# A fused attention and softplus feed-forward kernel: a list scheduler in place of a hand-interleaved order, and three weight phases in place of two

## The chip, the cores and the metric

The kernel runs on one core of a Trainium2 chip. The metric is the device time of one execution in microseconds: the median of the kernel's runs. The profiled execution is one more run, taken by the hardware profiler; its span goes from the first to the last instruction.

The engines are called by these names: TensorE (PE in the profile, PEld for its weight loads), VectorE (DVE), ScalarE (ACT), GpSimd (POOL) and SyncE (SP), which here only issues DMAs. Each engine works through its own instructions in program order and waits on semaphores for the others.

## The reference

```python
# q, k, v: (8, 8, 576, 64) float32; g_norm: (64,)
kv  = np.einsum('bhsd,bhse->bhde', k, v)
out = np.einsum('bhsd,bhde->bhse', q, kv)
rms = np.sqrt(np.mean(out * out, axis=-1, keepdims=True) + 1e-06)
x   = (out / rms * g_norm).transpose(0, 2, 1, 3).reshape(4608, 512)
# w_in: (512, 2048), w_out: (2048, 512), both float64
h   = x @ w_in
g   = np.maximum(h, 0.0) + np.log1p(np.exp(-np.abs(h)))   # softplus
return (g @ w_out).astype(np.float32)
```

The attention is linear: one 64 x 64 matrix kv for each batch and head, then q times it, and a norm over the 64 elements of a head.

## The kernel before

**Attention.** The 4608 tokens are 36 tiles of 128. For each of the 8 batches, `kv_part` (L240) accumulates k^T v of two heads at a time over the batch's 4.5 tiles in one PSUM bank; the two diagonal blocks are copied to `kv_diag`. For each tile, `turn_q` transposes q on TensorE (tp, L251) and ScalarE copies it out (qT, L253); `rows_out` (o, L262) multiplies it with `kv_diag`, ScalarE squares (L266), VectorE sums (L268), GpSimd raises to the power -1/2 (L269, L270), and `rows_norm` scales (L275). `turn_x` transposes the result (xp, L281), ScalarE multiplies it by g_norm (xg, L283), and x^T is stored in DRAM.

**Feed-forward.** Tokens are taken in 12 blocks of 384, d_ff in 16 chunks of 128. Each fp32 operand is divided into factors that TensorE multiplies in its fast fp32r mode: three for x^T (`split_x`, xv, L295 to L297), three for each weight (`divide` or `redivide`), three for g. A *step* is one chunk of one block: mm1 (L353) makes 128 x 384 of h with 12 matmuls; ScalarE computes softplus and the first factor (L358, L359), VectorE the other two (L360, L361): this is gv; mm2 (L373) adds gv's product with w_out to three sums of 128 x 512, one PSUM bank each, with 9 matmuls. There are 12 x 16 = 192 steps.

**Weights.** They arrive as float64. `conversion` makes fp32 of them in 128 x 512 halves (for each chunk a w_in half, j even, and a w_out half, j odd): six instructions of VectorE and three of ScalarE, then `divide`: one more on VectorE, three on ScalarE, and on TensorE the pair wd (L177, L178). Only eight chunks' factors fit in SBUF. So there are two phases of eight chunks: the first goes over all blocks with chunks 0 to 7, and leaves its sums in DRAM (ot, L379, the store L381); the second reads x^T and those partial sums again (L302, L390), adds them (L384) and writes the output (L386). Chunks 8 to 15 are converted during the first phase, spilled to DRAM, reloaded at the phases' turn and divided there by `redivide`.

**What sets the order.** Everything is written out by hand with `manual_schedule`. `attention` and `conversion` are generators; the main code advances them by given counts between the steps. While the first block's eight steps run, they start at fixed places among the conversions of the sixteen halves (`STARTS`, L440: step 0 with half 5, step 7 with half 15); after that each step advances the attention and the second half's conversions by one or two pieces. mm2 follows mm1 by `LAG = 2` steps. PSUM has two banks for mm1 and wd (tag h), three sums, and three banks (tag a) that kv, tp, o and xp share; when the attention is done, these three become a second set of sums (`ps_b`).

Of the kernel before, what the change touches and what calls it, by code (L numbers as in the profile page):

```python
# [8 lines left out]
F32 = mybir.dt.float32  # L9
# [9 lines left out]
P = 128  # L19
# [5 lines left out]

@with_exitstack
def kernel(
# [20 lines left out]

    nc = tc.nc
# [10 lines left out]
    CH = KF // 2  # L60
    LAG = 2
# [3 lines left out]
    wts = ctx.enter_context(tc.tile_pool(name="wts", bufs=1))  # L65
    dram = ctx.enter_context(tc.tile_pool(name="dram", bufs=1, space=DRAM))
    xpool = ctx.enter_context(tc.tile_pool(name="xpool", bufs=2))
    gpool = ctx.enter_context(tc.tile_pool(name="gpool", bufs=3))
    tmp = ctx.enter_context(tc.tile_pool(name="tmp", bufs=2))
    ps_h = ctx.enter_context(tc.tile_pool(name="ps_h", bufs=2, space=PSUM))  # L70
    ps_o = [ctx.enter_context(tc.tile_pool(name="ps_o", bufs=1, space=PSUM))]
    first_stack = ExitStack()
    ps_a = first_stack.enter_context(tc.tile_pool(name="ps_a", bufs=3, space=PSUM))
    att = first_stack.enter_context(tc.tile_pool(name="att", bufs=2))
    conv = first_stack.enter_context(tc.tile_pool(name="conv", bufs=1))

    ident_r = const.tile([P, P], F32R, name="ident_r")
    minus_r = const.tile([P, P], F32R, name="minus_r")
    ident = ident_r.bitcast(F32)
# [7 lines left out]

    wide = moe_w_in.dtype != F32
    raws, w_in_r, w_out_r, w_spill = {}, {}, {}, {}
# [11 lines left out]
    def fetch(j):  # L101
        src = w_source(j)
        dt, words = (U32, 2) if wide else (F32, 1)
        raws[j] = conv.tile([P, d_model, words], dt, tag="raw", bufs=2, name="raw")
        nc.sync.dma_start(
            out=raws[j].rearrange("p n w -> p (n w)").rearrange("p (a f) -> p a f", a=src.shape[1]), in_=src)

    def conversion(js, end):
# [8 lines left out]
        js = list(js)  # L117
        last = iter(())
        for j in js:
            raw = raws[j]  # L120
            w = conv.tile([P, d_model], F32, tag="w", name="w")
            if wide:
                lo, hi = raw[:, :, 0], raw[:, :, 1]
                t, p = (conv.tile([P, d_model], U32, tag=n, name=f"c_{n}") for n in "tp")
                tf, pf = t.bitcast(F32), p.bitcast(F32)
                lf = conv.tile([P, d_model], F32, tag="lf", name="lf")
                sq, junk = (conv.tile([P, d_model], BF16, tag=n, name=n) for n in ("sq", "junk"))
                nc.scalar.activation(sq, raw.bitcast(BF16)[:, :, 3], func=AF.Square, scale=2.0 ** 47)
                nc.scalar.activation(lf, lo, func=AF.Copy, scale=2.0 ** -52)
                nc.vector.tensor_scalar(out=t, in0=hi, scalar1=3, scalar2=0x3FFFFFF8,  # L130
                                        op0=ALU.logical_shift_left, op1=ALU.bitwise_and)
                yield
                nc.vector.scalar_tensor_tensor(out=t, in0=hi, scalar=0xC0000000, in1=t,
                                               op0=ALU.bitwise_and, op1=ALU.bitwise_or)
                raws.pop(j)
                if j + 2 <= js[-1]:
                    fetch(j + 2)
                yield
                yield from last
                nc.vector.scalar_tensor_tensor(out=tf, in0=sq, scalar=2.0 ** 64, in1=tf, op0=ALU.is_ge, op1=ALU.mult)  # L140
                nc.scalar.activation(junk, sq, func=AF.Identity, scale=2.0 ** -126, bias=big,
                                     accum_out=over[:, j:j + 1])
                yield
# [384 lines left out]
```

## Time and profile before

| | before |
|---|---|
| median of 3 runs | 1051.72 us (1051.38 to 1051.89) |
| the profiled execution's own time | 1047.91 us |
| its span | 1046.0 us |
| TensorE busy | 959.1 us, 92% |
| VectorE, ScalarE busy | 518.5 us, 424.8 us |
| DMA | 110.18 MB, 105 GB/s over the span |

A row of the groups reads: line, engine, operation, what is written <- what is read, shapes, count | busy us in all, mean ns of one | idle time of the engine just before them, and who ended it. One fp32 matmul is two instructions for kv and o (hence x8 for four matmuls), and one for the others. A row of a table by stretches reads: from and to in us, length, then busy us and instructions of TensorE, its weight loads, VectorE, ScalarE and GpSimd, TensorE's granted clock, the share of time in which the DMA engines moved data, and GB/s. The page's GB/s row gives equal slices of the span or of the window asked for.

### The profile page before, as it was taken

To read this page: it belongs to the slowest core of one execution; us is meant where nothing else is said; L and a number is where in the kernel's file an instruction comes from. 1 tells how busy PE (TensorE), PEld (TensorE's weight loads), DVE (VectorE), ACT (ScalarE), POOL (GpSimd) and SP (SyncE) were. 2 spreads that over 40 slices of the span, in tenths; PEclk is the share of its full clock that TensorE was granted. 3 is DMA by queue.
4 is the path that set the end of the run, shared out by engine and by line. 5 is a ranking of instruction groups with operands and counts; after the bars stand their busy time and mean duration, and the time that the engine had idled before them with its cause. 6 is when DMAs were issued, how large, how long until landed. Compare 5 with 4: busy or idle time off the path is not lost. (4 is left out here: it accounts for less than half of the span.)

```text
span 1046.0 us, 13139 instructions
## 1 busy us (share of the span) xinstructions
PE 959.1 (92%) x4994; PEld 861.4 (82%) x4994; DVE 518.5 (50%) x892; ACT 424.8 (41%) x834; POOL 88.3 (8%) x78
## 2 busy tenths in 40 slices
PE   4756768999998999989999999999999999999998
PEld 3646557898897978879898999899999999999997
DVE  3656754455464554546543457544443544444432
ACT  2546654444344443444532369333222322232221
POOL 0121112022021111113100000000000000000000
PEclk8587888999999999999999999999999999999999
DMA  9855544545555364443220333122211222022210
GB/s 220 186 151 137 139 121 121 153 121 161 143 139 143 99 161 117 126 119 104 100 65 16 101 114 108 52 90 91 81 51 51 91 91 81 25 77 91 81 61 31
DMA packets 158767, 110.18 MB, mean 105 GB/s; under 512 B 117104, under 2 KB 125296, under 8 KB 158704
## 3 DMA queue, kind: packets, MB, share of 16 engines
q1 hardware_dynamic: 158704, 109.34, 37.6%
q8 instruction: 39, 0.64, 0.3%
q14 instruction: 24, 0.20, 0.1%
HBM read 76.81 MB, written 32.51 MB: 105 GB/s over the span
## 5 line engine op out<-in xcount | busy, mean ns | idle before, releaser
L373 PE MATMUL op<-w,gv 128*128 128x512 f32 x1728 | 440.0, 398 | 11.2 <-ACT ot L379 11.2
L353 PE MATMUL hp<-xv,w 128*128 128x384 f32 x2304 | 439.5, 339 | 0.4 <-ACT g L358 0.4
L353 PEld LDWEIGHTS hp<-xv,w 128*128 128x128 f32 x2304 | 412.6, 189 | 16.6 <-ACT g L358 0.9
L373 PEld LDWEIGHTS op<-w,gv 128*128 128x128 f32 x1728 | 319.1, 189 | 73.2 <-ACT ot L379 14.2
L360 DVE TENSOR_TENSOR gv<-g,gv 128x384 fp32r<-128x384 f32 x192 | 107.1, 558 | 449.5 <-ACT gv L359 447.9
L358 ACT ACTIVATE g<-hp 128x384 f32<-128x384 f32 x192 | 94.1, 490 | 472.1 <-PE hp L353 470.6
L361 DVE SCALAR_TENSOR_TENSOR gv<-gv 128x384 fp32r<-128x384 f32 x192 | 107.2, 558 | 6.7
L359 ACT ACTIVATE gv<-g 128x384 fp32r<-128x384 f32 x192 | 100.8, 525 | 6.0
L270 POOL TENSOR_TENSOR r<-r,half 128x8 f32<-128x8 f32 x36 | 70.6, 1962 | 3.0
L240 PE MATMUL kv<-v_t,k_t 128*128 128x128 f32 (+1 forms) x320 | 55.1, 328 | 12.4 <-DMA v_t<-in_v_dram 12.4
L240 PEld LDWEIGHTS kv<-v_t,k_t 128*128 128x128 f32 (+1 forms) x320 | 51.1, 237 | 15.7 <-issue 13.8
L269 POOL TENSOR_SCALAR r<-r 128x8 f32<-128x8 f32 x36 | 17.0, 472 | 421.0 <-DVE r L268 421.0
L297 DVE SCALAR_TENSOR_TENSOR xv<-xv 128x512 fp32r<-128x512 f32 x72 | 49.8, 692 | 2.5
L262 PE MATMUL o<-kv_diag,qT 128*128 128x128 f32 (+1 forms) x320 | 46.3, 304 | 2.0 <-DVE sq L275 2.0
L296 DVE TENSOR_TENSOR xv<-xt,xv 128x512 fp32r<-128x512 f32 x69 | 47.3, 685 | 1.9 <-ACT xv L295 1.5
L262 PEld LDWEIGHTS o<-kv_diag,qT 128*128 128x128 f32 (+1 forms) x320 | 43.5, 205 | 4.1 <-DVE sq L275 2.5
L295 ACT ACTIVATE xv<-xt 128x512 fp32r<-128x512 f32 x69 | 42.8, 620 | 0.0
L178 PE MATMUL wd<-w,minus_r 128*128 128x512 f32 x16 | 10.8, 672 | 33.6 <-ACT w L174 33.6
L268 DVE TENSOR_REDUCE r<-sq 128x8 f32<-128x512 f32 x36 | 24.5, 681 | 28.8 <-ACT sq L266 28.5
L379 ACT ACTIVATE ot<-op 128x512 f32<-128x512 f32 x36 | 20.3, 593 | 43.9 <-DMA part<-ot 43.9
L251 PE MATMUL tp<-ident_r,q_t 128*128 128x128 f32 x144 | 25.5, 308 | 13.4 <-ACT xg L283 13.4
L178 PEld LDWEIGHTS wd<-w,minus_r 128*128 128x128 f32 x16 | 4.0, 250 | 38.8 <-ACT w L174 38.8
(50 smaller groups left out, 479.4 us busy)
## 6 DMA issues: line engine op xcount, KB each, us to landing
xt<-x SPq DMA_DIRECT2D x69, 256.0 KB, 2.8
x<-xg SPq DMA_DIRECT2D x36, 256.0 KB, 2.2
part<-ot SPq DMA_DIRECT2D x36, 256.0 KB, 2.2
pt<-part SPq DMA_DIRECT2D x36, 256.0 KB, 3.8
out_dram<-ot SPq DMA_DIRECT2D x36, 256.0 KB, 2.1
raw<-in_moe_w_in_dram SPq DMA_DIRECT2D x16, 512.0 KB, 4.6
k_t<-in_k_dram SPq DMA_DIRECT2D x32, 256.0 KB, 3.5
v_t<-in_v_dram SPq DMA_DIRECT2D x32, 256.0 KB, 4.2
```

The source lines that it names most:

```text
L240: nc.tensor.matmul(kvs[b][:, p], lhsT=kts[t][r0:r0 + n, 2 * p:2 * p + 2].rearrange("r h d -> r (h d)"), rhs=vts[t][r0:r0 + n, 2 * p:2 * p ...
L262: nc.tensor.matmul(o[r0:r0 + n, 2 * p:2 * p + 2].rearrange("r h d -> r (h d)"), lhsT=qT[:, p, r0:r0 + n], rhs=kv_diag[b % 2][:, p], start= ...
L270: nc.gpsimd.tensor_tensor(out=r, in0=r, in1=half, op=ALU.pow)
L295: nc.scalar.activation(xv[:, 0], x, func=AF.Copy, scale=DOWN)
L296: nc.vector.tensor_tensor(out=xv[:, 1], in0=x, in1=f32[:, 0], op=ALU.subtract)
L297: nc.vector.scalar_tensor_tensor(out=xv[:, 2], in0=f32[:, 1], scalar=-RADIX, in1=f32[:, 0], op0=ALU.mult, op1=ALU.add)
L353: nc.tensor.matmul(hp, lhsT=w[:, i, kd * P:(kd + 1) * P], rhs=xv[:, i, kd], start=(m == 0), stop=(m == 3 * KD - 1))
L358: nc.scalar.activation(g, hp, func=AF.Softplus, scale=1.0 + E)
L359: nc.scalar.activation(gv[:, 0], g, func=AF.Copy, scale=DOWN)
L360: nc.vector.tensor_tensor(out=gv[:, 1], in0=g, in1=f32[:, 0], op=ALU.subtract)
L361: nc.vector.scalar_tensor_tensor(out=gv[:, 2], in0=f32[:, 1], scalar=-RADIX, in1=f32[:, 0], op0=ALU.mult, op1=ALU.add)
L373: nc.tensor.matmul(sums[i], lhsT=gv[:, m, i * P:(i + 1) * P], rhs=w[:, m], start=(first and m == 0), stop=(last and m == 2))
```

## The change

The whole kernel is written as *tasks*. A task has an engine, an estimated duration in ns, the tasks that it comes after, a position `pos` (mostly a step's number, plus or minus a lead), and the buffer slots that it takes and gives back. `Plan.order` then lists them: at each turn it finds for every engine the ready tasks whose buffers are free, lets the one with the lowest position go among those that could start within 150 ns of the first, and takes the engine whose task starts earliest by the estimates. The tasks are emitted in order of those starts. Buffers are rings with fixed counts; a slot's place in its ring is picked by the plan. The order on each engine is then fixed in the program, as before.

Beside the order, these things change:

- Three phases of 4, 6 and 6 chunks. x^T is read back and split in each (108 splits of a tile in place of 72), and partial sums leave after phases 0 and 1 and are added in phases 1 and 2. Eight places for chunks' factors remain; chunks 4 to 7 and 10, 11 are divided straight from their conversion, 8, 9 and 12 to 15 are spilled and reloaded.
- Only chunks 0 to 3 use the wd pair on TensorE; the others' third factor is made by one more VectorE instruction.
- x^T of the first six tiles (two blocks in place of one) goes straight into its split.
- PSUM: two banks h, two banks o (for kv and o), one bank tp (for both transposes), and three sums s0, s1, s2, for the whole kernel.
- The addition of 1e-6 moves from GpSimd to VectorE (the factor 1/64 goes into the square); g_norm's two small loads go to ScalarE's queue, and minus_r is made by ScalarE.

The core of the diff (the conversion's six VectorE and three ScalarE instructions are the same, each now an `add` of its own):

```diff
+class Plan:
+    HANDOVER = {"PE": 250, "ACT": 120, "DVE": 120, "POOL": 150, "SP": 0}
+    SOON = 150
...
+    def order(self):
...
+            for engine, tasks in ready.items():
+                options = []
+                for t in tasks:
+                    at = max(engine_free[engine], t.ready)
+                    if t.size:
+                        at = max(at, dma_free - 2500)
+                    for s in t.take:
+                        if not free[s.ring]:
+                            break
+                        at = max(at, min(free[s.ring])[0])
+                    else:
+                        options.append((at, t))
...
+                first = min(at for at, _ in options)
+                at, t = min(((at, t) for at, t in options if at <= first + self.SOON),
+                            key=lambda o: (o[1].pos, o[0]))
+                if best is None or at < best[0]:
+                    best = (at, t)
...
-    CH = KF // 2
-    LAG = 2
+    PHASES = [range(0, 4), range(4, 10), range(10, 16)]
+    PLACES = 8
+    LAST = len(PHASES) - 1
+    AT_ONCE = 2 * TB
...
+    rings = dict(xv=2, gv=3, g=2, raw=2, lf=1, sq=1, junk=1, t=1, p=1, w=1,
+                 xt=2, kvt=6, q=2, qT=2, x=2, xg=2, r=2,
+                 h=2, o=2, tp=1, s0=1, s1=1, s2=1)
+    rings.update({f"w{i}_{c}": 1 for i in range(2) for c in range(PLACES)})
...
+        def less():
+            nc.vector.scalar_tensor_tensor(out=w.tile, in0=d.tile, scalar=-RADIX, in1=dst.tile.bitcast(F32)[:, 0],
+                                           op0=ALU.mult, op1=ALU.add)
...
+        a = add("PE", 440, turn_q, [ld], pos - 1, [tp], [q_s])
...
+        a = add("PE", 440, turn_x, [a], pos + 0.5, [xp], [x])
...
+        if t < AT_ONCE:
+            split(0, t, xg, a, pos + 0.5)
...
+        a = mm1s[s] = add("PE", 2100, mm1, x_split[ph, n] + factors_done[0, c] + [mm1s.get(s - 1)], s, [h],
+                ([xv] if c == cs[-1] else []) + ([w_in] if s == last_step[c] else []))
...
+            a2 = add("PE", 700, lambda i=i: mm2(i), [a] + factors_done[1, c] + [mm2s.get(i)], s + 1.5,
+                     [mine[i]] if c == cs[0] else [],
+                     [gv] + ([w_out] if s == last_step[c] else []))
...
+            pt = slot("kvt")
+            ld = add("SP", 350, lambda: nc.sync.dma_start(out=new(pt, [P, d_model]), in_=part[ph - 1, t][0]),
+                     [part[ph - 1, t][1]], pos - 3, [pt], [], 1200, behind=int(pos) - 4)
+            a = add("DVE", 700, lambda: nc.vector.scalar_tensor_tensor(
+                out=new(ot, [P, d_model]), in0=bank.tile, scalar=(scale if ph == LAST else 1.0 + E), in1=pt.tile,
+                op0=ALU.mult, op1=ALU.add), [done, ld] + (scale_done if ph == LAST else []), pos, [ot], [bank, pt])
...
+    for t in plan.order():
+        t.run()
```

**TensorE at the start.** Before, from just ahead of the first mm1 (hp; wd, tp, kv, o and xp are as above):

```order
L281 MATMUL xp<-ident_r,sq 128x128 x4
L353 MATMUL hp<-xv,w_0_167 128x384 x12
L177 MATMUL wd<-w_2_524,ident_r 128x512
L178 MATMUL wd<-w_2_524,minus_r 128x512
L251 MATMUL tp<-ident_r,q_t 128x128 x4
L240 MATMUL kv<-v_t,k_t 128x128 x4
L262 MATMUL o<-kv_diag_97,qT 128x128 x4
L353 MATMUL hp<-xv,w_1_274 128x384 x12
```

Now, at the same place. L523 is mm1, L341 and L342 the wd pair in a bank h, L455 tp, L435 kv (in a bank o):

```order
L435 MATMUL o_354<-kvt_483,kvt_478 128x128 x4
L523 MATMUL h_541<-xv_446,w_0_0_251 128x384 x12
L455 MATMUL tp_568<-ident_r,q_495 128x128 x4
L523 MATMUL h_575<-xv_446,w_1_0_401 128x384 x12
L341 MATMUL h_604<-w_2_0_560,ident_r 128x512
L342 MATMUL h_604<-w_2_0_560,minus_r 128x512
L455 MATMUL tp_610<-ident_r,q_511 128x128 x4
L523 MATMUL h_620<-xv_446,w_2_0_560 128x384 x12
```

Before, the first block's mm1s stand one or two to a chunk among eight chunks' wd pairs and the attention's pieces; now four chunks' do, and block 1's first mm1 follows 45 of TensorE's rows after this first one.

**TensorE at a block's turn.** Before, in the second phase: the last chunk's mm1 (w_7), then the next block's, and mm2 (L373) two chunks behind:

```order
L353 MATMUL hp<-xv,w_7_5534 128x384 x12
L373 MATMUL op_5829<-w_5_5436,gv 128x512 x3
L373 MATMUL op_5833<-w_5_5436,gv 128x512 x3
L373 MATMUL op_5837<-w_5_5436,gv 128x512 x3
L353 MATMUL hp<-xv,w_0_5186 128x384 x12
L373 MATMUL op_5829<-w_6_5482,gv 128x512 x3
```

Now, in phase 1, whose chunks are 4 to 9 (8 and 9 stand in places 0 and 1). L530 is mm2:

```order
L523 MATMUL h_5339<-xv_5022,w_1_0_3692 128x384 x12
L530 MATMUL s_0_5197<-w_0_0_3747,gv_5333 128x512 x3
L530 MATMUL s_0_5207<-w_0_0_3747,gv_5333 128x512 x3
L530 MATMUL s_0_5240<-w_0_0_3747,gv_5333 128x512 x3
L523 MATMUL h_5369<-xv_5260,w_4_0_914 128x384 x12
L530 MATMUL s_0_5197<-w_1_0_3789,gv_5363 128x512 x3
L530 MATMUL s_0_5207<-w_1_0_3789,gv_5363 128x512 x3
L530 MATMUL s_0_5240<-w_1_0_3789,gv_5363 128x512 x3
L523 MATMUL h_5404<-xv_5260,w_5_0_1485 128x384 x12
L530 MATMUL s_0_5426<-w_4_0_1216,gv_5391 128x512 x3
L530 MATMUL s_0_5436<-w_4_0_1216,gv_5391 128x512 x3
L523 MATMUL h_5443<-xv_5260,w_6_0_2055 128x384 x12
```

mm2 now stands one step behind mm1, not two, and at the turn an mm1 stands ahead of the third sum's first mm2.

**SyncE at a block's turn.** Before, in the second phase (xt: x^T read back; pt: a partial sum read back; out_dram: the output's store):

```order
L302 DMA xt<-x_737 128x512
L390 DMA pt<-part_1430 128x512
L390 DMA pt<-part_1437 128x512
L390 DMA pt<-part_1444 128x512
L302 DMA xt<-x_893 128x512
L386 DMA out_dram<-ot 128x512 x3
```

Now, in phase 1, over two blocks' ends. L574 stores a sum, L568 loads the partial sums (into kvt buffers), L308 spills a weight, L246 fetches one:

```order
L574 DMA part_17_191<-qT_5231 128x512
L568 DMA kvt_5244<-part_18_156 128x512
L568 DMA kvt_5249<-part_19_157 128x512
L568 DMA kvt_5256<-part_20_158 128x512
L501 DMA xt_5285<-x_100 128x512
L308 DMA w_spill_133<-w_5319 128x512
L246 DMA raw_5356<-in_moe_w_in_dram 128x4x256
L574 DMA part_18_192<-qT_5393 128x512
L574 DMA part_19_193<-qT_5420 128x512
```

The loads of a block's partial sums stood between the loads of x^T, shortly ahead of that block's stores; now they stand right behind the stores of the block before, with a spill and a fetch between them and their own block's stores.

More of the change, by code (lines that the diff above doesn't have):

```diff
@@ new lines, in split, with x_pos @@
+        before = x_split.get((ph, n), [None])[-1:]
+        a = add("ACT", 640, high, [ready] + ([] if i == 0 else [first_high[ph, n]]), pos, [dst] if i == 0 else [])
+        if i == 0:
+            first_high[ph, n] = a
+        b = add("DVE", 700, low, [a], pos, [], [x])
+        c = add("DVE", 700, less, [b], pos)
+        x_split.setdefault((ph, n), []).append(c)
+    first_high = {}
+    k_slots, v_slots, k_ready = {}, {}, {}
+    kv_ready = {}
+    o_tasks = {}
+    def x_pos(t):
+        n = t // TB
+        return t - 12 if n == 0 else first_step[0, n] - (5 if n == 1 else 7) + t % TB
```

688 lines of the change are left out of this document (362 added, 326 removed).

## The prediction

> **What bounds the kernel now.** I read the page's busy shares first, then the busy time in four stretches of the span.
>
> ```profile
> PE 959.1 (92%) x4994; PEld 861.4 (82%) x4994; DVE 518.5 (50%) x892; ACT 424.8 (41%) x834; POOL 88.3 (8%) x78
> core 0: us, PE busy (x) PEld busy (x) DVE busy (x) ACT busy (x) POOL busy (x), PEclk, DMA share, GB/s
> 0.00:200.00 200.00, 135.69 (x666) 116.78 (x667) 109.49 (x191) 102.36 (x197) 33.16 (x34) 0.81 0.65 155
> 200.00:500.00 300.00, 284.67 (x1621) 257.63 (x1621) 157.09 (x273) 131.92 (x263) 50.22 (x41) 0.99 0.47 129
> 500.00:656.00 156.00, 153.00 (x780) 138.38 (x779) 82.98 (x143) 78.87 (x156) 4.91 (x4) 1.00 0.26 85
> 656.00:1046.00 390.00, 385.80 (x1931) 348.56 (x1930) 168.95 (x286) 111.63 (x219) 0.00 (x0) 1.00 0.21 69
> ```
>
> TensorE is the bound from 200 us on: idle for 300 - 284.67 = 15.3, then 3.0, then 4.2 us. In the first 200 us no engine is full, and TensorE's granted clock is 0.81. To price that stretch I need TensorE's whole work at full clock. The chain that ended last gives the step (one mm1 and one mm2), since it is TensorE alone there:
>
> ```profile
> 665.54 2.10 PE hp L353 x12
> ...
> 1033.97 2.10 PE hp L353 x12
> 1036.08 6.18 PE op L373 x27
> ```
>
> 88 steps lie between the first two rows: 368.43 / 88 = 4.187 us, and 192 steps make 803.9. The end is 1046.0 - 1036.08 - 6.18 = 3.7 us after the last matmul. The attention work is priced from the groups of TensorE between 200 and 500 us, at clock 0.99:
>
> ```profile
> L373 PE MATMUL op<-w,gv 128*128 128x512 f32 x486 | 127.6, 405 | 10.2 <-ACT ot L379 10.2
> L353 PE MATMUL hp<-xv,w 128*128 128x384 f32 x643 | 122.6, 339 | 0.0
> L262 PE MATMUL o<-kv_diag,qT 128*128 128x128 f32 (+1 forms) x176 | 22.3, 277 | 0.0
> L240 PE MATMUL kv<-v_t,k_t 128*128 128x128 f32 (+1 forms) x152 | 20.4, 277 | 0.0
> L251 PE MATMUL tp<-ident_r,q_t 128*128 128x128 f32 x84 | 12.9, 276 | 6.4 <-ACT xg L283 6.4
> L281 PE MATMUL xp<-ident_r,sq 128*128 128x128 f32 x80 | 12.1, 274 | 0.0
> ```
>
> 643/12 and 486/9 make 53.8 steps, 225.3 us. Of the 284.67 busy, 59.4 are left for (176 + 152)/8 = 41 groups of kv or o and (84 + 80)/4 = 41 groups of transposes. Shared out as their busy times (42.7 to 25.0) that is 0.915 us for a kv or o group and 0.535 for four transposes. The whole kernel has
>
> ```profile
> L240 PE MATMUL kv<-v_t,k_t 128*128 128x128 f32 (+1 forms) x320 | 55.1, 328 | 12.4 <-DMA v_t<-in_v_dram 12.4
> L251 PE MATMUL tp<-ident_r,q_t 128*128 128x128 f32 x144 | 25.5, 308 | 13.4 <-ACT xg L283 13.4
> L178 PE MATMUL wd<-w,minus_r 128*128 128x512 f32 x16 | 10.8, 672 | 33.6 <-ACT w L174 33.6
> ```
>
> 320/8 = 40 groups of kv and as many of o, 144/4 = 36 of each kind of transposes: 73.2 + 38.5 us. The 16 pairs of wd matmuls, each matmul as long as one of mm2 (6.18/27 = 0.23), are 7.4. TensorE's work is 803.9 + 73.2 + 38.5 + 7.4 = 923.0 us, so 123.0 us of the span are lost. Of these, 15.3 + 3.0 + 4.2 lie after 200 us; **100 us are lost in the first 200**.
>
> What the first 200 us wait for is the weights: sixteen chunk halves are converted before the first block can end, and the groups of VectorE up to 150 us show what one costs.
>
> ```profile
> L148 DVE TENSOR_TENSOR w<-c_t,c_p 128x512 f32<-128x512 f32 x14 | 9.7, 690 | 0.3
> L173 DVE TENSOR_TENSOR d<-w,w 128x512 f32<-128x512 f32 x14 | 9.6, 685 | 0.0
> L268 DVE TENSOR_REDUCE r<-sq 128x8 f32<-128x512 f32 x10 | 6.9, 685 | 24.4 <-ACT sq L266 24.4
> L130 DVE TENSOR_SCALAR c_t<-raw 128x512 uint32<-128x512 uint32 x15 | 6.4, 425 | 12.8 <-DMA raw<-in_moe_w_out_dram 9.4 <-DMA raw<-in_moe_w_in_dram 3.1
> L297 DVE SCALAR_TENSOR_TENSOR xv<-xv 128x512 fp32r<-128x512 f32 x5 | 3.5, 692 | 0.2
> L360 DVE TENSOR_TENSOR gv<-g,gv 128x384 fp32r<-128x384 f32 x6 | 3.3, 558 | 12.7 <-ACT gv L359 12.7
> ```
>
> Two instructions of L130's kind and five of L148's and L173's: 2 x 0.425 + 5 x 0.69 = 4.3 us for a half, 69 us for sixteen. VectorE is idle between them, behind the rows' releasers.
>
> **The change, part by part.** *Four chunks in the first phase.* Eight halves are needed before block 0 can end in place of sixteen: 34 us of VectorE work leave the start; the other halves are spread over later steps. Eight wd pairs go (3.7 us): TensorE's work is now 919.3.
>
> *A listed order.* I count what stands ahead of block 1's first mm1 in the new order. VectorE: nine halves (38.7), seven tiles' reduce, add and norm (about 1.43 each, 10.0), six x splits (2 x 0.69 each, 8.3), four gv pairs (4.5), three kv copies and the memsets (3.5): 65 us. TensorE: 24 groups of kv or o (22.0), 17 of transposes (9.1), eight wd pairs (3.7), four steps (16.7): 51.5 us at full clock. DMA up to the last k and v of the third batch: 38 loads of k, v or q of 0.26 MB and 5.8 MB of weights and x. The queues' view of the first 50 us shows the rates:
>
> ```profile
> GB/s 0 0 41 297 304 220 218 218 218 218 217 218 217 249 359 358 226 233 292 292 218 217 218 193 37 291 306 232 210 183 197 28 56 323 284 175 69 199 144 120
> q1 hardware_dynamic: 28907, 10.10, 98.0%
> ```
>
> At 217 GB/s for the first kind (the long flat stretch) and some 330 for the rest: 46 + 17 us, from 3.8 us on, so 67. VectorE's first conversion began at 5.99 us and ends these 65 us at 71 if it never waits. At the 55% that it is busy over the first 200 us now it would be at 125; at the best ten microseconds of the first hundred, 69%, at 100:
>
> ```profile
> 5.99 0.43 DVE L130 TENSOR_SCALAR c_t<-raw 128x512 uint32<-128x512 uint32 x1 [3.11 <-DMA raw<-in_moe_w_in_dram]
> 90.00:100.00 10.00, 5.56 (x23) 4.65 (x23) 6.89 (x13) 6.95 (x13) 1.43 (x2) 0.66 0.27 78
> ```
>
> I take 86, the middle of 71 and 100: the new order is listed by when things are ready, while the old one interleaves generators by hand, but VectorE, ScalarE and DMA now all need 65 to 70 us there. Loss at the start: 86 - 51.5 = 34.5 (19.5 to 73.5).
>
> *The rest of phase 0.* TensorE has 919.3 - 51.5 - 144 x 4.187 = 264.9 us of work. The stretch 200:500 holds the same mixture and loses 15.3 on 284.7, 5.4%: 14 us. The ends are 0 (the stretch from 656 on loses next to nothing before its end) and 34: the transposes now have one bank, so each of the 55 groups still to come may wait for ScalarE's copy of the one before, 0.58 or 0.68 us.
>
> ```profile
> L253 ACT COPY qT<-tp 128x512 f32<-128x512 f32 x36 | 20.7, 575 | 5.7 <-PE tp L251 5.6
> L283 ACT ACTIVATE xg<-xp,g_col 128x512 f32<-128x512 f32 x36 | 24.4, 676 | 2.4 <-DMA x<-xg 2.2 <-PE xp L281 0.3
> ```
>
> *Three phases instead of two.* x is split 36 times more (1.38 us of VectorE each) and 36 more partial sums leave and are added again:
>
> ```profile
> L384 DVE SCALAR_TENSOR_TENSOR ot<-op,scale,pt 128x512 f32<-128x512 f32 x36 | 24.8, 743 | 2.6 <-PE op L373 2.6
> pt<-part SPq DMA_DIRECT2D x36, 256.0 KB, 3.8
> ```
>
> That is 49.7 + 26.8 = 76 us of VectorE, 27 MB of traffic. I cost it at nothing: it falls where VectorE is busy for 169 of 390 us and DMA for 0.21, beside TensorE. Without that cover it would cost the 76.
>
> *Lag of one, one set of sum banks.* mm2 of a step now follows mm1 of the next one; before, two further. How long gv takes is seen in the steady state:
>
> ```profile
> 799.70 1.92 PE L353 MATMUL hp<-xv,w 128*128 128x384 f32 x10
> 801.66 0.49 ACT L358 ACTIVATE g<-hp 128x384 f32<-128x384 f32 x1 [2.62 <-PE hp L353]
> 803.33 0.56 DVE L361 SCALAR_TENSOR_TENSOR gv<-gv 128x384 fp32r<-128x384 f32 x1
> ```
>
> From mm1's end (799.70 + 1.92 = 801.62) to gv's (803.89) are 2.27 us; the cover is one mm2 and one mm1, 4.19, so 1.9 us are spare. An eviction (0.74) or half a split (0.69) in the way fits; three evictions and a half split (2.9) miss by 1.0. Over the 24 turns of the later phases that is 0 to 24 us; I take 4, since the listed order sets the evictions between the gv pairs. g_col's loads on ScalarE's queue, minus_r there and the addition moved from POOL to VectorE (0.06 each) cost nothing: ScalarE's first work waits for the raw weights until 5.99 anyway.
>
> **Sum**: 919.3 + 34.5 + 14 + 4 + 3.7 = 975.5 us of span. The profiled execution took 1047.91 for a span of 1046.0, and the median, 1051.72, is 3.8 above it: 975.5 + 1.9 + 3.8 = **981 us**. All the low ends give 948, all the high ones 1060.
>
> **Rivals.** *The clock stays at half over the start.* A kv group takes either of two lengths:
>
> ```profile
> 31.32 1.91 PE L240 MATMUL kv<-v_t,k_t 128*128 128x128 f32 x8
> 54.15 1.06 PE L240 MATMUL kv<-v_t,k_t 128*128 128x128 f32 x8
> ```
>
> Between them TensorE waits for the weights' conversion, up to 5.3 us at a time:
>
> ```profile
> PE wd L178 <- ACT w L174: 33.6, 12, 5.3
> ```
>
> If TensorE does its 51.5 us at half rate it needs 103, from 8.5 on: block 1 starts at 112, 26 later than I take, **1007**. Against it: more work in fewer microseconds leaves fewer gaps. The Trainium skill (TensorE: Matmul & The Clock Gate, "HAM oscillation — how this bites in real kernels") says that gaps beyond some 3.4 us bring the half rate back; the trace's longest wait ahead of wd, with the 0.81 of that stretch, agrees, and by that rule this rival is what happens if such gaps stay.
>
> *Lone banks.* The three sum banks are all there are, now in the later phases too. If at each of those 24 turns TensorE sits through three evictions, 2.2 us, it costs 53 in place of my 4: **1030**. For it: the old kernel's 10.2 us behind ot between 200 and 500, in its phase with one set. Against it: the new order lets an mm1 pass ahead of the third sum. The Trainium skill (Perfetto Trace Analysis, "Optimizing Tensor Performance") advises to rotate independent groups through different banks so that evacuation overlaps; by that advice this rival is the outcome, and the old trace's tiny loss after 656 with two sets fits it.
>
> *Loads behind stores (slower).* SyncE's queue is in order, and a store in it waits for its eviction. If the partial sums' loads come to stand so late that each of the 24 turns waits for a landing, 3.8 us, that adds 91: **1072**. It decides when a load is issued less than 3.8 us before its block's last mm2. Against it: the listed queue has those loads a block ahead.
>
> *It does nothing*: the start is held by something that no order changes, **1052**. The first 50 us at 98% DMA speak for it; that the first 200 have a mean of 0.65, so 0.54 after the 50, speaks against.
>
> **How the numbers follow.** Forecast 0.75 (its own range 952 to 1012), half clock 0.09, lone banks 0.08, no effect 0.02, loads behind stores 0.06. The range 950 to 1024 takes in the forecast's and the clock's, and leaves out the other three and the tails. A difference under 0.2% (2 us) can't be told from none. Faster 0.92, same 0.02, slower 0.06.
>
> **What would show it.** Block 1's first mm1 near 86 us, and VectorE busy for three quarters until then; the clock at 1.0 from about 100 us; the first phase over near 365; after that a step of 4.19 us with gaps under 0.3 us at the turns. Wrong if block 1 starts after 110, if TensorE waits over 1 us at most turns, or if VectorE or SyncE's queue turns up as the releaser of mm2 after the first phase.

## The result, and the profile after

The kernel takes **949.35 us** (median of 4 runs, 948.73 to 950.03) against 1051.81 for the kernel before, run beside it (4 runs): a ratio of 0.902 (0.9005 to 0.9038), 102 us less. The forecast was 981, 32 us too long. The profiled execution took 948.73 us.

The busy shares on the page of the changed kernel:

```profile
PE 920.4 (97%) x4978; PEld 834.2 (88%) x4978; DVE 596.5 (63%) x1043; ACT 443.7 (47%) x871; POOL 66.6 (7%) x42
```

Its busy time by stretches (columns as explained above; L530 is mm2, L523 mm1, L461 o, L435 kv, L455 and L477 the two kinds of transposes):

```profile
0.00:50.00 50.00, 31.96 (x189) 27.99 (x190) 34.98 (x65) 32.56 (x62) 7.90 (x10) 0.93 1.13 241
50.00:100.00 50.00, 46.66 (x302) 41.64 (x301) 41.40 (x76) 36.08 (x70) 12.31 (x8) 1.00 0.77 187
100.00:200.00 100.00, 100.00 (x639) 91.53 (x638) 73.05 (x132) 64.32 (x126) 21.05 (x12) 1.00 0.82 220
200.00:400.00 200.00, 200.00 (x1135) 182.68 (x1134) 136.22 (x242) 114.24 (x224) 25.37 (x14) 1.00 0.53 163
400.00:947.00 547.00, 541.75 (x2721) 490.37 (x2719) 310.90 (x531) 196.48 (x390) 0.00 (x0) 1.00 0.33 109
```

TensorE is never idle between 100 us and its last matmul at 400 + 541.75 = 941.75. Where the old kernel lost 100 us in its first 200, this one loses 18.0 of the first 50 and 3.3 of the next. All of TensorE's waits that the trace names lie ahead of 60 us; the largest are these (who waits, for whom: total us, times, longest):

```profile
PE o L435 <- DMA kvt<-in_v_dram: 11.4, 3, 9.0
PE tp L477 <- DVE x L472: 2.9, 3, 2.6
PE h L342 <- ACT w L330: 2.8, 3, 1.3
PE tp L455 <- DMA q<-in_q_dram: 1.4, 1, 1.4
```

The 33.6 us behind ScalarE's w, the largest wait before, are 2.8 now. The largest that remains is the landing of k and v, 9.0 of its 11.4 us ahead of the first. Block 1's first mm1, which I had put at 86 us, and phase 1's first, which I had put near 365, stand here in the timeline:

```profile
80.67 2.33 PE L523 MATMUL h<-xv,w 128*128 128x384 f32 x12
...
337.35 2.27 PE L523 MATMUL h<-xv,w 128*128 128x384 f32 x12
```

The groups between 100 and 300 us price the work, since no idle time is left there:

```profile
L530 PE MATMUL s<-w,gv 128*128 128x512 f32 x287 | 78.3, 406 | 0.0
L523 PE MATMUL h<-xv,w 128*128 128x384 f32 x384 | 73.9, 341 | 0.0
L461 PE MATMUL o<-kv_diag,qT 128*128 128x128 f32 (+1 forms) x216 | 27.0, 276 | 0.0
L435 PE MATMUL o<-kvt,kvt 128*128 128x128 f32 (+1 forms) x184 | 24.6, 276 | 0.0
L455 PE MATMUL tp<-ident_r,q 128*128 128x128 f32 x96 | 14.4, 272 | 0.0
L477 PE MATMUL tp<-ident_r,x 128*128 128x128 f32 x96 | 14.4, 272 | 0.0
```

The chain that ended last gives the step, 24 of them between its first and last row here, which are 100.34 us apart, 4.181 each:

```profile
823.96 2.76 PE s L530 x12
...
924.30 2.76 PE s L530 x12
```

32 steps make 133.6 of the 200 us; the other 66.4 are (216 + 184)/8 = 50 groups of kv or o and 48 of transposes. Shared out by busy time (51.6 to 28.8) that is 0.853 us and 0.496 for one, where I had 0.915 and 0.535 from the old kernel.

### The profile page after: what moved, and what is told of

It reads as the page before. It is cut to its first block, busy times and chain, and to the rows that moved or that the text cites. A ratio compares the mean times of both kernels' runs of the same rounds, so it can differ in the third digit from the quotient of the medians.

```text
span 946.9 us, 13479 instructions
## 1 busy us (share of the span) xinstructions
PE 920.4 (97%) x4978; PEld 834.2 (88%) x4978; DVE 596.5 (63%) x1043; ACT 443.7 (47%) x871; POOL 66.6 (7%) x42
## 4 chain that ended last, share of the span: by engine, by line
PE 94%; DVE 2%; DMA 1%; ACT 1%; issue 0%; SPq 0%; POOL 0%; DVEq 0%; POOLq 0%
PE s L530 42%; PE h L523 42%; PE o L435 4%; PE o L461 3%; PE tp L455 2%; PE tp L477 1%; DMA kvt<-in_v_dram 1%; DVE w L289 0%; DVE t L273 0%; DVE t L268 0%; DVE p L286 0%; DMA out_dram<-qT 0%; PE s L461 0%; POOL r L469 0%; DVE r L465 0%
## 5 line engine op out<-in xcount | busy, mean ns | idle before, releaser
L530 PE MATMUL s<-w,gv 128*128 128x512 f32 x1728 | 438.5, 396 | 0.0
L523 PE MATMUL h<-xv,w 128*128 128x384 f32 x2304 | 435.9, 337 | 0.1
L523 PEld LDWEIGHTS h<-xv,w 128*128 128x128 f32 x2304 | 406.0, 188 | 14.6 <-ACT g L543 0.4
L530 PEld LDWEIGHTS s<-w,gv 128*128 128x128 f32 x1728 | 318.1, 188 | 57.9 <-issue 0.5
L543 ACT ACTIVATE g<-h 128x384 f32<-128x384 f32 x192 | 94.5, 492 | 417.0 <-PE h L523 408.7
L401 DVE SCALAR_TENSOR_TENSOR xv<-xv 128x512 fp32r<-128x512 f32 x108 | 74.6, 691 | 2.9
L435 PE MATMUL o<-kvt,kvt 128*128 128x128 f32 (+1 forms) x320 | 45.7, 292 | 11.4 <-DMA kvt<-in_v_dram 11.4
L435 PEld LDWEIGHTS o<-kvt,kvt 128*128 128x128 f32 (+1 forms) x320 | 42.9, 204 | 14.9 <-issue 11.4
L570 DVE SCALAR_TENSOR_TENSOR qT<-s,scale,kvt 128x512 f32<-128x512 f32 x36 | 26.9, 749 | 37.3 <-PE s L530 29.8
L461 PE MATMUL o<-kv_diag,qT 128*128 128x128 f32 (+1 forms) x296 | 37.0, 276 | 0.0
L461 PEld LDWEIGHTS o<-kv_diag,qT 128*128 128x128 f32 (+1 forms) x296 | 34.6, 179 | 1.5 <-issue 0.3
L491 ACT ACTIVATE xg<-tp,g_col 128x512 f32<-128x512 f32 x36 | 24.7, 686 | 12.8 <-PE tp L477 12.3
L480 ACT COPY qT<-tp 128x512 f32<-128x512 f32 x36 | 21.0, 582 | 12.5 <-PE tp L455 12.2
```

Source lines behind the costliest of these rows:

```text
L401: nc.vector.scalar_tensor_tensor(out=cols(2, F32R), in0=cols(1), scalar=-RADIX, in1=cols(0), op0=ALU.mult, op1=ALU.add)
L435: nc.tensor.matmul(kv[:, p], lhsT=pairs(k_slots[t].tile[r0:r0 + n], p), rhs=pairs(v_slots[t].tile[r0:r0 + n], p), start=(i == 0 and p == 0 ...
L461: nc.tensor.matmul(pairs(y[r0:r0 + n], p), lhsT=qT.tile[:, p, r0:r0 + n], rhs=kv_diag[b % 2][:, p], start=(p == 0), stop=True, skip_group_ ...
L523: nc.tensor.matmul(hp, lhsT=w_in.tile[:, i, kd * P:(kd + 1) * P], rhs=xv.tile[:, i, kd], start=(m == 0), stop=(m == 3 * KD - 1))
L530: nc.tensor.matmul(mine[i].tile, lhsT=gv.tile[:, m, i * P:(i + 1) * P], rhs=w_out.tile[:, m], start=(c == cs[0] and m == 0), stop=(c == cs ...
L543: a = add("ACT", 490, lambda: nc.scalar.activation(new(g, [P, NT]), h.tile, func=AF.Softplus, scale=1.0 + E), [a], s, [g], [h])
```

## The experiments

Each time is a median; each ratio is to the kernel before, run on the same chip. "The changed kernel" is the one above.

**Two phases, the list and the rings as changed.**

```diff
-    PHASES = [range(0, 4), range(4, 10), range(10, 16)]
+    PHASES = [range(0, 8), range(8, 16)]
...
```

The positions of the weights of chunks 4 to 15 in the list move with the phases, and chunks 8 to 15 are all spilled.

> The changed kernel with two phases of eight chunks, as before, but the same list, rings and banks. Theory A (the listed order carries the gain: TensorE stops waiting because every engine's list follows readiness): the start gets longer by some of the eight halves' 34 us of VectorE, but the list can put attention and more steps into it, so 950 to 970 us. Theory B (fewer halves at the start carry it): block 0's end moves out by most of those 34 us, 975 to 990 us.

983.44 us, ratio 0.935 (0.932 to 0.938). By stretches:

```profile
0.00:50.00 50.00, 31.32 (x183) 27.92 (x184) 34.28 (x64) 32.35 (x61) 6.52 (x9) 0.93 1.03 226
50.00:100.00 50.00, 30.84 (x131) 23.35 (x129) 46.82 (x82) 40.06 (x79) 1.81 (x1) 0.86 0.34 100
100.00:150.00 50.00, 44.52 (x237) 39.76 (x238) 33.53 (x61) 25.59 (x48) 8.88 (x5) 0.93 0.42 111
150.00:980.00 830.00, 824.25 (x4431) 748.58 (x4429) 418.18 (x730) 333.84 (x649) 46.63 (x27) 1.00 0.36 105
```

The first 50 us are as before; then VectorE is full (46.82 of 50) with eight more halves, and TensorE waits. The 34 us that this costs equal the 34 of VectorE work that I had counted for eight halves; that VectorE's amount is the cause was not tested in this kernel. From 150 us on TensorE loses 5.75 us, nearly all of it behind its last matmul, so here too the first phase has no stalls left after its start. So a third of the gain is the phases', and two thirds (1051.8 - 983.4 = 68 us) are there without them. How the 68 divide between the list and the rest of the change (the PSUM banks, the wd pairs, x^T of two blocks straight) was not taken apart in full.

**Positions without times.** Tasks, rings and banks stay; `order` emits the ready task of lowest position whose buffers are free, and no time is estimated.

```diff
-                first = min(at for at, _ in options)
...
+            t = min(options, key=lambda o: (o.pos, index[id(o)]))
```

> The changed kernel's tasks, rings and phases, but emitted in order of position (the lowest position among the tasks whose inputs and buffers are there, no times), a stand-in for an order by hand. Theory A: the 5.4 per cent that the old first phase lost comes back and the start is less well packed: 965 to 1000 us, with TensorE waiting after 80 us. Theory B: 949 to 956 us.

1321.45 us, ratio 1.258 (1.251 to 1.265). TensorE's two largest waits:

```profile
PE tp L446 <- DVE x L441: 131.2, 33, 15.9
PE h L310 <- ACT w L292: 59.4, 8, 11.4
```

The positions alone are a worse order than the old one by hand, so this is no stand-in for that; it shows that the tasks, rings and positions give none of the gain without an order that suits them. With two phases as well:

> Both undone: two phases and order by position. If the two add, the losses of the two single runs against 949 us add up here; if the list is what makes the start short, this comes near the old 1052 us. Theory A: mostly e2's loss. Theory B: mostly e1's.

1238.44 us, ratio 1.177 (1.173 to 1.181). Here three phases lose 83 us to two, where they gain 34 with the times: the two effects don't add.

**x^T of one block straight, in place of two** (`AT_ONCE = TB`).

> Only the first block's x^T goes straight into its split; block 1's goes through DRAM. If the start is bound by VectorE and DMA volume: 0 to +2 us. If the round trip (a store and a load, 2.9 and 3.3 us to landing) lies on the path to block 1: +6 us or more.

956.42 us, ratio 0.909 (0.9066 to 0.9114). The stretch from 50 to 100 us loses 6.9 us in place of 3.3, the first 50 lose 1.8 more, and block 1's first mm1 comes at 91.69 us in place of 80.67. That fits a round trip through DRAM on block 1's path; the list was made anew, so part of it can be another order.

**What holds the start.** First the loads: k, v and q read as rows of 2 KB in place of 256-byte pieces, each engine's order unchanged.

```diff
-                nc.sync.dma_start(out=x[r0:r0 + n], in_=src[b, :, s0:s0 + n].rearrange("h s d -> s h d"))
+                nc.sync.dma_start(out=x[r0:r0 + n], in_=rows[t * P + r0:t * P + r0 + n])
```

> k, v and q are read as if they lay in rows of 2 KB in place of 256-byte pieces: the attention is computed on other elements, with the same instructions in the same order on every engine. It takes the 217 GB/s plateau out of the start. Theory D (DMA sets the start): TensorE's 21 us of idle time before 60 us shrink by about half, 935 to 942 us. Theory V (VectorE sets it, busy 9.6 of 10 us from 30 to 60): the loads come earlier but block 1 does not, 946 to 950 us.

947.54 us, ratio 0.902 (0.8995 to 0.904): no difference that can be told. The queues' view of the first 50 us, of the changed kernel and then of this one:

```profile
GB/s 0 65 320 349 207 274 218 217 218 217 218 218 218 217 211 219 305 272 314 310 222 283 304 224 305 312 227 214 243 167 226 258 201 218 262 273 306 233 220 350
q1 hardware_dynamic: 31229, 12.01, 112.6%
```

```profile
GB/s 0 62 309 280 188 256 406 405 364 92 339 26 84 266 179 366 321 276 331 251 169 356 323 16 184 370 298 197 72 151 241 313 207 275 136 194 342 374 28 164
q1 hardware_dynamic: 6868, 11.48, 71.5%
```

The plateau at 217 GB/s is gone and the queues have slack, but TensorE's wait for the first v stays (11.1 us): DMA volume is not the bound.

Then VectorE: the first eight halves without the low words, in a freshly listed order,

> The first eight halves leave out the low words of the weights: two of VectorE's seven instructions go (1.1 us a half, 8.9 us in all), nothing else. Theory V: block 1 starts 6 to 9 us earlier, 940 to 944 us. Theory D: 947 to 950 us.

951.01 us, ratio 0.904 (0.902 to 0.906); and with a third buffer for raw weights, and with the third and fourth halves fetched ahead of most of k, v and q too (TensorE and VectorE are listed anew in both):

```diff
-    rings = dict(xv=2, gv=3, g=2, raw=2,
+    rings = dict(xv=2, gv=3, g=2, raw=3,
...
-                pos = -18.0 + 0.8 * j if j < 2 else -13 + 1.6 * j
+                pos = -18.0 + 0.8 * j if j < 4 else -13 + 1.6 * j
```

> Three buffers for the raw float64 weights in place of two; the third and fourth halves stand at nearly the same place in the queue behind the first k, v and q, the fifth and sixth come earlier. The first wait of VectorE for raw weights (8.2 us up to 22.6 us) stays; the later ones, 1.8 us in all, go. If the start is bound by a mixture of chains: no change, 946 to 952. If the later raw weights set block 1's start: 2 us less, 945 to 948.

> Three raw buffers, and the third and fourth halves are fetched ahead of most of the first k, v and q. VectorE's gap of 8 us up to 22.6 us should close by some 6 us. If that gap sets block 1's start (VectorE needs a fixed amount of work until then and lost these 8 us): block 1's first mm1 moves from 80.7 to 75 us and the kernel takes 943 to 945 us. If k, v and q, which now land some 5 us later, are the longer chain: 949 to 956 us, with longer waits of the first kv matmuls for their loads.

954.27 us (0.907, 0.9054 to 0.9094) and 951.89 us (0.905, 0.903 to 0.906). Neither is better than the changed kernel. In the second, the fetch that VectorE waited 8.2 us for at 22.6 is early, and block 1's first mm1 still comes late, at 85 us. But all three move the order as well. So two more keep the order of every engine and only shorten VectorE's work (16 columns in place of 512 in two instructions of each of the first eight halves), alone and with the 2 KB rows:

> The first eight halves keep all their instructions and the listed order of every engine, but two of VectorE's (the power of two and its product with the low words) work on 16 columns of 512, and the sum that follows takes the high words alone: the low words of chunks 0 to 3 are left out of the result. VectorE's work at the start falls by some 8 x 0.9 = 7 us at an unchanged order. If VectorE's amount sets the start: block 1's first mm1 comes 5 to 7 us earlier, 942 to 945 us. If the loads and the round trips of each tile set it: within 2 us, 947 to 951.

> The same, and k, v and q are read as whole rows of 2 KB in place of 256-byte pieces (other elements of the inputs, so the attention is of permuted data), again with the same order on every engine. If the start is held by VectorE and the loads in turn, each hiding what the other would give: 936 to 942 us here, though either alone gave nothing or little. If it is held by neither (by the chains from TensorE to ScalarE and back in the order as listed): 946 to 951.

949.89 us (0.903, 0.902 to 0.9045) and 948.2 us (0.902, 0.900 to 0.903). By stretches, the changed kernel and then the one with VectorE's work alone shortened:

```profile
30.00:60.00 30.00, 22.39 (x152) 18.97 (x151) 28.84 (x51) 26.21 (x52) 7.21 (x4) 1.00 1.06 243
```

```profile
30.00:60.00 30.00, 23.14 (x139) 20.28 (x139) 25.40 (x52) 25.96 (x52) 7.26 (x4) 0.92 0.99 225
```

VectorE has 6.9 us less to do in the first 100 and no time comes of it: block 1's first mm1 stands at 82.51. The granted clock is lower in the second row (0.92), which could hide some 2 us (8% of 30), not the 5 to 7 that I had expected. In the changed kernel block 0's first mm1 is at 42.80 and block 1's at 80.67; in the last of these runs they are at

```profile
40.48 2.33 PE L527 MATMUL h<-xv,w 128*128 128x384 f32 x12
...
78.60 2.33 PE L527 MATMUL h<-xv,w 128*128 128x384 f32 x12
```

Between the two lie 37.9 us there and 38.1 here: less VectorE work and faster loads together leave this stretch as it is. Block 1 starts 2.1 us earlier, but its start moves almost as much between executions of one order: in two other runs whose order on TensorE and ScalarE is the same up to there (the tail's buffers and the added VectorE work, below) it is at 82.22 and 82.32. The theories that VectorE's amount or the loads' rate set the start both fall, and so does the one that each hides the other (7 to 13 us expected); 2 to 4 us of such an effect can't be excluded.

**The end.** The last phase's sums leave through three kinds of buffers in turn, not two places of one (in the last phase the ring of `ot` is `("qT", "xg", "x")[t % TB]`).

> The output's last sums leave through three buffers (of the rings qT, xg and x, idle then) in place of two of qT. In the changed kernel's trace the third waits 1.5 us for the first one's store at the very end. Expected: 1.4 us less at the end, 948 us; if the stores themselves are what ends last, no change.

949.03 us, ratio 0.902 (0.9004 to 0.9043). In the time it can't be told, but the timelines show the effect: VectorE's last eviction in the changed kernel, and here:

```profile
943.33 0.75 DVE L570 SCALAR_TENSOR_TENSOR qT<-s,scale,kvt 128x512 f32<-128x512 f32 x1 [1.47 <-DMA out_dram<-qT]
```

```profile
943.68 0.75 DVE L570 SCALAR_TENSOR_TENSOR x<-s,scale,kvt 128x512 f32<-128x512 f32 x1
```

The wait of 1.47 us for a store is gone, and the span ends 3.66 us after TensorE in place of 5.15. A slower start in this one execution (its TensorE ended 1.9 us later) hides it.

**Phases of 3, 6 and 7 chunks.**

> Phases of 3, 6 and 7 chunks. Theory B in numbers (each half that must be ready before block 0 can end costs VectorE's 4.3 us at the start, as the 34 us of the two-phase run for eight halves say): two halves fewer, 940 to 942 us. If the bound of the start is elsewhere, or VectorE or ScalarE, now fuller in a shorter first phase (36 steps), make TensorE wait after 80 us: 948 us or more.

966.67 us, ratio 0.919 (0.917 to 0.921): slower than 4, 6 and 6 by 17, where I had expected faster.

```profile
50.00:100.00 50.00, 44.92 (x280) 40.64 (x279) 29.56 (x54) 26.94 (x50) 13.36 (x8) 0.86 0.80 200
100.00:200.00 100.00, 95.60 (x617) 86.23 (x616) 75.37 (x136) 65.13 (x127) 23.91 (x13) 1.00 0.85 225
200.00:300.00 100.00, 96.99 (x587) 86.55 (x586) 81.54 (x147) 71.75 (x141) 21.54 (x12) 1.00 0.73 218
```

TensorE now has idle time to 300 us, 7.4 of it between 100 and 300. Between 50 and 100 us VectorE is busy for 30 of 50 and ScalarE for 27: no engine is full there. Of TensorE's waits between 100 and 300 the trace puts 4.5 us behind the attention's copies (qT, xg, x) and 2.1 behind evicted sums. That three steps of a block don't cover the chain of the attention's pieces, and four do, would fit, but is not shown: the edit also lists the next six chunks' conversions closer together (a half every 2.5 steps in place of 3 to 3.5), and the two were not separated. The granted clock of 0.86 in the first row is part of the loss.

**More VectorE work later.** One more VectorE instruction of 128 x 512 in each of the 144 steps of phases 1 and 2.

> Each of the 144 steps of phases 1 and 2 gets one more VectorE instruction on 128 x 512 elements of a buffer of its own (some 0.69 us each, 99 us in all, more than the 76 us that the three phases brought); its result is used nowhere. VectorE was busy for 60% of the time from 400 us on, and would now be busy for some 77%. If VectorE's added work is hidden behind TensorE there (the term of nothing in the prediction): 947 to 953 us. If it lies in the way of the evictions and of gv at the 24 turns (a turn has some 1.9 us to spare, three evictions and a half split already need 2.9): up to 24 turns x 0.7 to 2 us, 966 to 995. If it is all on the path: 1048.

950.22 us, ratio 0.903 (0.9014 to 0.9049): nothing, for 84 us more of VectorE (680.4 busy in place of 596.5).

**The turns.** The first edit meant to keep each mm1 behind the mm2 two steps before it, but chained it to the step just before, as the diff shows, so it measures another thing than its expectation says:

```diff
-                [mm1s.get(s - 1)], s, [h],
+                [mm1s.get(s - 1), mm2s.get(2)], s, [h],
```

> Each mm1 now also comes after all three parts of mm2 that stand two steps before it, so that TensorE's order in the steps is fixed as mm1, three mm2, mm1, three mm2; the listed kernel lets an mm1 pass ahead of the third sum's first mm2 at a turn. If the mm1 ahead is what covers the lone sum banks (the rival of lone banks): the third sum's eviction ends some 1.5 to 3.5 us after its last mm2, of which one mm1 and two parts of mm2, 3.5 us, are covered anyway; at 34 turns 0 to 1 us each, plus gv's delay where evictions stand ahead of it on VectorE, gives 955 to 985. If the banks have slack without it: 947 to 953. The start may lose some, since the third and later mm1 can't run ahead of mm2 there; that would show before 80 us.

1400.09 us, ratio 1.330 (1.3275 to 1.333). With no mm1 between, every step waits for its own gv:

```profile
1003.05 2.25 PE L523 MATMUL h<-xv,w 128*128 128x384 f32 x12
1006.43 4.23 PE L530 MATMUL s<-w,gv 128*128 128x512 f32 x9 [1.14 <-ACT gv L545]
1007.01 0.56 DVE L538 SCALAR_TENSOR_TENSOR gv<-gv 128x384 fp32r<-128x384 f32 x1
```

And one stretch of it:

```profile
800.00:1200.00 400.00, 322.31 (x1235) 241.43 (x1234) 134.51 (x221) 88.71 (x171) 0.00 (x0) 0.92 0.19 62
```

From mm1's end (1005.30) to gv's end (1007.57) are 2.27 us, the prediction's number. That one mm1 and one mm2 hide it in the changed kernel is what this run shows by losing the cover. The loss a step is not the same quantity, though: it is (1400.09 - 949.35) / 192 = 2.35 us on the average, but 2.6 between 800 and 1200 us (1235 matmuls are 58.8 steps of 6.8 us), and part of that is the granted clock, 0.92 there and 1.00 in the changed kernel. That 2.35 lies near 2.27 is in part chance. The edit that was meant:

```diff
-                [mm1s.get(s - 1)], s, [h],
+                [mm1s.get(s - 1), sum_done.get(s - 2)], s, [h],
```

> What the run before meant to be: mm1 now comes after the last part of mm2 two steps before it, so that no mm1 passes ahead of any part of mm2, and a turn is mm1, three mm2, mm1, three mm2 like every other step (the listed kernel splits one group of three in three or four). If the mm1 that passes ahead covers the lone sum banks: the third sum must be evicted in the 3.5 us of one mm1 and two parts of mm2, and VectorE has gv and splits in between; 34 turns of 0.5 to 2 us, and the attention's transposes lose some of their places: 966 to 1015. If fixed places are as good: 947 to 955.

961.9 us, ratio 0.915 (0.913 to 0.918), 12.5 more than the changed kernel. By stretches:

```profile
0.00:100.00 100.00, 76.63 (x451) 67.76 (x452) 73.03 (x135) 65.56 (x126) 18.77 (x16) 0.91 0.87 201
100.00:300.00 200.00, 199.19 (x1262) 181.98 (x1263) 143.25 (x260) 127.20 (x247) 43.32 (x24) 1.00 0.78 212
300.00:900.00 600.00, 596.64 (x2997) 538.12 (x2996) 359.86 (x609) 240.53 (x471) 3.62 (x2) 1.00 0.35 114
```

TensorE's two largest waits from 100 us on:

```profile
PE s L531 <- DVE qT L571: 2.6, 3, 1.3
PE s L531 <- ACT xg L565: 0.9, 3, 0.4
```

From 100 to 900 us TensorE loses 4.2, of which 3.5 are behind evictions, in six waits: that is what the mm1 that passes ahead saves at the turns. The rest is spread. Phase 1's first mm1 comes 8.3 us later (345.69 in place of 337.35), with 2.0 of idle time more ahead of 100 us at a granted clock of 0.91, where the changed kernel has 0.97; what makes up the remainder was not followed up.

**The planner's times.** Without the handovers and the 2 us of a landing (the durations kept), and with 600 ns for every task:

```diff
-    HANDOVER = {"PE": 250, "ACT": 120, "DVE": 120, "POOL": 150, "SP": 0}
+    HANDOVER = {"PE": 0, "ACT": 0, "DVE": 0, "POOL": 0, "SP": 0}
...
-                t.end = dma_free + 2000
+                t.end = dma_free
```

> The planner's estimates keep each task's duration, but no time passes between one engine's end and another's start (was 120 to 250 ns), and a transfer counts as landed when its queue has moved it (was 2 us later). If the order hangs on the durations alone: 947 to 956. If it hangs on these small times, because the listed order then puts a reader at the first moment at which it could start: 960 to 1000, with many short waits of TensorE for VectorE and ScalarE and longer ones for loads.

> The planner takes every task for 600 ns long (mm1 was 2100, GpSimd's power 2000, the smallest 100); handovers and transfers keep their estimates. If only the positions and the buffers' counts matter, and any plan of times keeps the engines apart: 950 to 970. If the durations carry the order: the plan sees a step of TensorE as 2.4 us in place of 4.2, and VectorE as the bound for long stretches, so that mm1 comes ahead of attention pieces or the reverse: 990 to 1150, most of the loss before 300 us.

968.9 us (0.922, 0.919 to 0.925) and 994.34 us (0.946, 0.9435 to 0.9487). The small times are worth 20 us: TensorE is busy for 72.7 of the first 100 us (78.6 in the changed kernel), and loses 7.4 from there to 900. With equal durations, TensorE between 100 and 400 us, where the changed kernel is busy for 300:

```profile
100.00:400.00 300.00, 274.24 (x1596) 241.69 (x1595) 185.13 (x330) 165.90 (x323) 46.78 (x27) 0.98 0.62 172
```

And its two largest waits from 100 us on:

```profile
PE s L530 <- ACT xg L564: 8.0, 8, 2.8
PE tp L455 <- ACT xg L491: 6.0, 6, 2.2
```

These are of the kinds of the old kernel's two waits between 200 and 500 us, 10.2 behind the evicted sum (then ot, now an xg buffer) and 6.4 behind xg. With the same tasks, buffers and positions they come and go with the durations by which the list is made.

## Why the prediction was too long

| term | forecast | measured |
|---|---|---|
| TensorE's work | 919.3 | 910.4 |
| loss at the start | 34.5 | 30.5 |
| rest of phase 0 | 14 | 0 |
| turns | 4 | 0 |
| after the last matmul | 3.7 | 5.2 |
| span | 975.5 | 946.1 by these terms (946.9) |
| execution over span, median over execution | 1.9 + 3.8 | 1.8 + 0.6 |

The work is 192 x 4.181 + 80 x 0.853 + 72 x 0.496 + 3.7 = 910.4. The start's loss is 80.67 less the work ahead of it by these prices, 25 x 0.853 + 17 x 0.496 + 3.7 + 4 x 4.181 = 50.2; the trace has 25 groups of kv or o there (200 matmul instructions), one more than I had counted. The places in time agree with the table: phase 1 starts 28 us ahead of the forecast (337.35 against 365), and 22 of these 28 come between block 1's start and there.

**The step that failed** is "*The rest of phase 0*": "The stretch 200:500 holds the same mixture and loses 15.3 on 284.7, 5.4%: 14 us." A stall was carried over as if it went with the mixture of work. It goes with the order: with the same tasks and buffers, the run with equal durations has 25.8 us of idle time in the 300 from 100 to 400, the changed kernel none. The low end of that term, 0, was given, and was right; the value that I took was not. The same stretch also gave the prices of attention work: 7.8 us too much for 152 groups. A granted clock of 0.99 is in them, and perhaps stalls too short to be shown as idle; which of the two weighs more is not shown. The last 3.8 us, from the profiled execution to the median, came from one execution of the old kernel and were 0.6 here. Together with the turns (4), the start (4), the step (1) and the longer end (-1.5) that is the whole difference to within 1 us. That the sum of all the low ends, 948, comes out near the measured time is chance: the start's loss was 11 us above its low end, and the work, for which no low end was given, 8.9 below its value.

**The start** came out at 80.67 where I took 86, near enough, but not for the reason given. VectorE was busy for 76.4 of the first 100 us, as forecast; yet with 6.9 us less of its work block 1 starts no earlier (82.51). By TensorE's own rows the 30.5 us are 21.4 of idle time, 9.0 of them ahead of the first k and v, and 9.1 of work at less than the full rate (it was busy for 59.3 us to do 50.2). From 60 us on it is full, so the last 20 us ahead of block 1 are set by TensorE's own list. Which chain sets the waits between 9 and 60 us, 12.4 in all, was not settled and stays open.

**Three phases** at nothing was right: 84 us of VectorE work more, on top of the 76, cost nothing. Their gain of 34 us came out as counted, but the reason that I gave for it, 4.3 us of VectorE's time for each half, is not shown: it would have made 3, 6 and 7 chunks faster, and they were 17 us slower, in a run that also moved the conversions. **Lag of one**: the 2.27 us are confirmed. Its 4 us at the turns are of the size that the order with fixed places loses (4.2 from 100 to 900 us, 3.5 of them in six waits, not a little at each of 24 turns); the list's mm1 ahead of the third sum takes them away.

**The rivals.** *Half clock*: the granted clock is 0.93 in the first 50 us and 1.00 from then on, and block 1 starts at 81, not 112. The rows show the lower rate early, also ahead of 14 us, where the clock's column has 1.00:

```profile
11.76 1.91 PE L435 MATMUL o<-kvt,kvt 128*128 128x128 f32 x8
...
16.38 1.05 PE L435 MATMUL o<-kvt,kvt 128*128 128x128 f32 x8
18.64 1.13 PE L435 MATMUL o<-kvt,kvt 128*128 128x128 f32 x8 [1.21 <-DMA kvt<-in_v_dram]
21.15 0.90 PE L455 MATMUL tp<-ident_r,q 128*128 128x128 f32 x4 [1.38 <-DMA q<-in_q_dram]
23.27 3.09 PE L435 MATMUL o<-kvt,kvt 64*128 64x128 f32 x16 [1.22 <-DMA kvt<-in_v_dram]
26.31 2.94 PE L461 MATMUL s<-kv_diag,qT 128*128 128x128 f32 x16
29.52 1.16 PE L461 MATMUL s<-kv_diag,qT 128*128 128x128 f32 x8 [0.27 <-ACT qT L480]
```

```profile
20.00:30.00 10.00, 7.36 (x40) 6.55 (x41) 6.03 (x11) 5.15 (x11) 0.00 (x1) 0.66 1.21 279
```

Eight matmul instructions take 1.91 us at 11.76 and 1.05 at 16.38; sixteen take 2.94 at 26.31, eight 1.16 at 29.52, and the granted clock is 0.66 from 20 to 30: the rate had fallen back, though no wait since 9 us was longer than 1.4. The run with each mm1 chained to the mm2 before it has 0.92 from 800 to 1200 us with no wait longer than 1.14. The Trainium skill (TensorE: Matmul & The Clock Gate, "HAM oscillation — how this bites in real kernels") ties the fall to gaps beyond some 3.4 us; by that rule alone these matmuls would have run at the full rate, and the measurement differs. *Lone banks*: no idle time is left ahead of mm2, and none of the 53 us came. The Trainium skill (Perfetto Trace Analysis, "Optimizing Tensor Performance") advises to rotate groups through different banks; here one set of three loses nothing where an mm1 is listed into the eviction, and 3.5 us where none may be. *Loads behind stores*: TensorE waits for no load after 60 us. *It does nothing*: refuted by 102 us.

## What to carry to other kernels

A stall seen in the old profile belongs to the order that made it: when a change replaces the order, price the bounding engine's work from a stretch without idle time, and carry a stall over only with its releaser and a reason why the new order keeps it. A list made from estimated times is worth as much as its durations: the same tasks gave 949 us with them, 994 with equal ones, and 1321 with positions alone (the list alone was not set against the old order by hand). Less work on an engine that is busy but not the bound gave nothing that could be told here, even where it was 96% busy; shorten it at an unchanged order before you believe that it sets the pace.

## What was not expected of the hardware

Loads in 256-byte pieces ran at 217 to 218 GB/s for long stretches and at up to 406 as rows of 2 KB, with no difference to the time that could be told here. The small addition that moved to VectorE (128 x 8) takes 0.17 us, not the 0.06 that I had for it; 36 of them, hidden.
